# Reordering the last stage of an attention plus soft-mixture kernel: second-layer parts, their sums, output products and the copies between them

## The chip, the cores and the metric

The kernel runs on one core of one Trainium2 chip. The metric is the device time of one execution in microseconds (us), the median over repeated runs. The profile is that of one execution; its engines are PE (TensorE matmul), PEld (TensorE weight load), DVE (VectorE), ACT (ScalarE), POOL (GpSimd) and SP (SyncE), and 16 DMA engines move data between HBM and the core.

## The reference: what is computed

First an attention in both directions between 512 tokens and 32 states, for 8 batches and 8 heads of width 64; its results, 544 rows for each batch, make the 4608 x 512 matrix `x` of a soft mixture of experts:

```python
logits = x @ phi                        # 4608 x 32: 8 experts, 4 slots each
d = softmax of logits over the rows;  slot_input = d.T @ x      # 32 x 512
for e in range(8):
    h = np.maximum(slot_input[e] @ w1[e], 0.0)     # 4 x 1024
    slot_out[e] = h @ w2[e]                        # 4 x 512
c = softmax of logits over the 32 slots
return c @ slot_out                     # 4608 x 512
```

All data are 32-bit floats. `w1` and `w2` are 16 MB each, the tokens 8 MB, the output 9 MB.

## The kernel before, in words

The tokens and the weights are loaded whole, by 1 MB transfers that the SP engine issues one after the other on one queue, as buffers of the pool `big` come free. The attention stage is a long list of steps in a fixed order. Then come the experts. The first layer (`w1_part`, L679) issues the last weight transfers as it goes (`load_w`, `load_w2`, L115).

The change lies in what follows, the second layer and the output. The order in which PE, ACT, DVE and SP get their instructions is the order in which the steps are called, written by hand in the last block of the listing. Each engine takes its own instructions in that order and waits where an operand is not there.

- The 512 output columns fall into four parts `k` = 0 to 3 of 128 columns. Parts 0 and 1 need the weight tiles of half `c` = 0, parts 2 and 3 those of half `c` = 1, and the tiles of `c` = 1 arrive last. `more(k, n)` issues the next `n` of the 16 pieces of part `k`; a piece (`w2_part`, L745) is four matmuls for one expert and one half of the hidden width, and stands in the trace as 8 matmul records. All pieces of a part add up in one PSUM bank of the pool `ps_s`, which has two banks.
- `so_copy(k)` (L758) takes the finished part from PSUM to `so_sb`. `so_sum(k)` is one matmul (L763) that adds up four row groups, and an ACT copy of its result to `so_r` (L764).
- `out(k, q)`, for `q` = 0 and 1, makes four products of 128 x 512 (L774, 8 matmul records in all) in four PSUM banks, two of `ps_m` and two of `ps_t`; both pools have three banks. ACT copies the products 0 and 2 (L783), DVE the products 1 and 3 (L784), and SP sends the 1 MB tile to HBM, in one transfer (L789), or in two of 512 KB, each after its pair of copies (L787), for those in `HALVED`.
- `out_st(c)` (L796 to L805) does the same for the 256 KB of state rows of one half.

The queue of the transfers is the same for loads and stores: SP issues an output transfer after it has issued everything called before it and when the copies are done.

Of the kernel before, what the change touches and what calls it, by code (L numbers as in the profile page):

```python
# [8 lines left out]
F32 = mybir.dt.float32  # L9
# [6 lines left out]
P = 128  # L16
# [6 lines left out]
NJ = S // P  # L23
# [41 lines left out]
def attention_soft_moe(ctx: ExitStack, tc: tile.TileContext, x0, x, stT, phi, w1, w2, out_x, out_s):  # L65
# [7 lines left out]
    pe, act, dve, pool = nc.tensor, nc.scalar, nc.vector, nc.gpsimd  # L73
# [20 lines left out]
    for b in range(1, B):  # L94
        t = big.tile([P, 4, NJ, 2 * D], F32, tag="big", name=f"x{b}")
# [70 lines left out]
    with ExitStack() as actx:  # L166
        wk = actx.enter_context(tc.tile_pool(name="work", bufs=1))
        sm = actx.enter_context(tc.tile_pool(name="small", bufs=2))
        ps_s = actx.enter_context(tc.tile_pool(name="ps_s", bufs=2, space=PSUM))
        ps_t = actx.enter_context(tc.tile_pool(name="ps_t", bufs=3, space=PSUM))  # L170
        ps_m = actx.enter_context(tc.tile_pool(name="ps_m", bufs=3, space=PSUM))
# [10 lines left out]
        def half(name):  # L182
            return wk.tile([P, S], F32, tag="h", name=name, bufs=NH)
# [528 lines left out]
        c = [half(f"c{i}") for i in range(3)]  # L712
        c = [v[:, 0 : t.shape[1]].rearrange("p (t n) -> p t n", n=NS) for v, t in zip(c, c_t)]
# [23 lines left out]
        so, so_sb, so_r = {}, {}, {}  # L737
        PART = {k: (k // 2, P * (k % 2), P) for k in range(4)}

        def w2_part(k, hf, e):  # L740
            c, col, n = PART[k]
            if hf == 0 and e == 0:
                so[k] = ps_s.tile([P, n], F32, tag="sc", name=f"so_ps{k}")
            for i in range(4):
                pe.matmul(  # L745
                    so[k][32 * i : 32 * i + 32, :],
                    h_m[hf][:, 256 * i + 32 * e : 256 * i + 32 * e + 32],
                    w2t[c, e, 4 * hf + i][:, col : col + n],
                    start=(hf == 0 and e == 0),
                    stop=(hf == 1 and e == E - 1),  # L750
                )

        def so_copy(k):
            c, col, n = PART[k]
            if col == 0:
                so_sb[c] = half(f"so_sb{c}")[:, 0:256]
                so_r[c] = half(f"so_r{c}")[:, 0:256]
            dve.tensor_copy(so_sb[c][:, col : col + n], so[k])  # L758

        def so_sum(k):  # L760
            c, col, n = PART[k]
            p = ps_m.tile([P, n], F32, tag="ms", name=f"sum_ps{k}")
            pe.matmul(p, rep, so_sb[c][:, col : col + n], start=True, stop=True)  # L763
            act.copy(so_r[c][:, col : col + n], p)  # L764

        HALVED = ((0, 0), (3, 1))

        def out(k, q):
            hf, col = k // 2, 128 * (k % 2)
            o = [(ps_t if j % 2 else ps_m).tile([P, 512], F32, tag="tr" if j % 2 else "ms", name=f"o{k}_{q}_{j}")  # L770
                 for j in range(NJ)]
            for j in range(NJ):
                rows = slice(32 * j, 32 * j + 32)
                pe.matmul(  # L774
                    o[j],
                    so_r[hf][rows, col : col + 128],
                    lt_all[rows, 4 * q : 4 * q + 4, :].rearrange("p b s -> p (b s)"),
                    start=True,
                    stop=True,
                )  # L780
            ot = big.tile([P, NJ, 512], F32, tag="big", name=f"out{k}_{q}")
            for jp in range(2):
                act.copy(ot[:, 2 * jp], o[2 * jp])  # L783
                dve.tensor_copy(ot[:, 2 * jp + 1], o[2 * jp + 1])  # L784
                if (k, q) in HALVED:
                    half_rows = slice(1024 * jp, 1024 * jp + 1024)
                    nc.sync.dma_start(out_x[k, q][:, half_rows], ot[:, 2 * jp : 2 * jp + 2].rearrange("p i s -> p (i s)"))  # L787
            if (k, q) not in HALVED:
                nc.sync.dma_start(out_x[k, q], ot.rearrange("p i s -> p (i s)"))  # L789
# [39 lines left out]
        def more(k, n):  # L829
            for _ in range(n):  # L830
                w2_part(*part[k].pop(0))
# [5 lines left out]
        more(1, 4)  # L837
        more(0, 8)
        so_copy(0)
        more(1, 4)  # L840
        so_sum(0)
        more(1, 2)
        out(0, 0)
        more(1, 4)
        out(0, 1)
        more(1, 2)
        so_copy(1)
        more(2, 3)
        so_sum(1)
        more(2, 2)  # L850
        out(1, 0)
        more(2, 5)
        out(1, 1)
        more(2, 6)
        so_copy(2)
        more(3, 3)
        so_sum(2)
        out(2, 0)
        more(3, 5)
        out(2, 1)  # L860
        more(3, 8)
        so_copy(3)
        out_st(0)
        so_sum(3)
# [32 lines left out]
```

## Time and profile before

| what | value |
|---|---|
| device time, median of 3 runs | 131.25 us (131.04 to 131.4) |
| device time of the profiled execution | 131.05 us |
| its span, first to last instruction | 129.3 us |
| PE, DVE, ACT, POOL busy | 90%, 68%, 59%, 35% of the span |
| moved by DMA | 51.76 MB, mean 400 GB/s |
| read from and written to HBM | 42.53 MB and 8.91 MB |

The device time is 1.75 us longer than the span; this part lies outside what the profile shows. The busy shares are means over the whole span. The stage that the change touches runs from about 97 us to the end, and from 122.8 us on no compute engine works: there only transfers are left.

### The profile page before, as it was taken

Reading aid. Unit: us, or ns where it says so; the run is one execution under the profiler, and the core shown is the slowest. Engines: PE = TensorE matmul, PEld = TensorE weight load, DVE = VectorE, ACT = ScalarE, POOL = GpSimd, SP = SyncE. Lnnn points to the kernel's source line nnn. Section 1 sums busy time; section 2 is a strip of 40 time slices with the busy share of each in tenths; the row PEclk is TensorE's granted clock in tenths of the full one; section 3 lists DMA queues with packets and bytes.
Section 4 is the critical chain, followed back from the end, with each engine's and each line's share of the span. In section 5 each row is a group of like instructions: output and inputs, shape, how many; then the busy total and the mean of one; then the engine's idle time right before and its main releaser. Section 6 shows DMA issues by size and latency. Waiting matters only on the chain.

```text
span 129.3 us, 4981 instructions
## 1 busy us (share of the span) xinstructions
PE 116.3 (90%) x2112; PEld 82.1 (64%) x2112; DVE 88.1 (68%) x224; ACT 76.8 (59%) x187; POOL 45.2 (35%) x64
## 2 busy tenths in 40 slices
PE   6888999999999999999889899999999989898800
PEld 3527676869596976858676768963497546575300
DVE  3049999999999999999997349208950536263800
ACT  3118999999999999988985930410100425162700
POOL 2205393294575339057967113901600000000000
PEclk9999999999999999999999999999999999999965
DMA  4999999999999999999999999999999999989695
GB/s 104 382 415 426 428 423 426 421 421 426 413 431 423 421 428 421 434 416 428 418 426 423 423 403 404 402 434 423 426 421 428 423 409 397 416 325 423 287 404 214
DMA packets 8806, 51.76 MB, mean 400 GB/s; under 512 B 976, under 2 KB 1104, under 8 KB 3408
## 3 DMA queue, kind: packets, MB, share of 16 engines
q1 hardware_dynamic: 8640, 50.93, 95.3%
q10 hardware_dynamic: 144, 0.52, 1.1%
q8 instruction: 16, 0.26, 0.7%
q14 instruction: 6, 0.05, 0.1%
HBM read 42.53 MB, written 8.91 MB: 398 GB/s over the span
## 4 chain that ended last, share of the span: by engine, by line
PE 52%; DVE 32%; ACT 4%; DMA 3%; issue 3%; DVEq 0%; ACTq 0%
PE h_ps L679 11%; PE so_ps L745 11%; PE o L774 7%; PE xt_ps L232 5%; DVE q L260 5%; DVE aT L290 4%; DVE l1s L276 4%; DVE m L265 4%; DVE nm L296 4%; DMA x_a<-x_in 3%; PE sc L247 3%; PE eT_ps L315 2%; PE sr_ps L340 2%; DVE r L281 2%; PE t_ps L489 2%
## 5 line engine op out<-in xcount | busy, mean ns | idle before, releaser
L269 POOL TENSOR_TENSOR q<-q,m 128x512 f32<-128x512 f32 x16 | 16.7, 1049 | 16.1 <-DVE m L265 7.6
L238 ACT ACTIVATE xt<-xt_ps 128x512 f32<-128x512 f32 x30 | 17.9, 619 | 6.8 <-PE xt_ps L232 6.7
L285 POOL TENSOR_TENSOR q<-q,r 128x512 f32<-128x512 f32 x16 | 16.7, 1048 | 8.3 <-DVE r L281 2.7
L784 DVE COPY out<-o 128x512 f32<-128x512 f32 x16 | 10.3, 686 | 11.6 <-PE o L774 11.6
L745 PEld LDWEIGHTS so_ps<-w,h_m 128*32 128x32 f32 x512 | 13.6, 110 | 5.6 <-issue 5.3
L745 PE MATMUL so_ps<-w,h_m 128*32 128x128 f32 x512 | 16.2, 274 | 0.0
L232 PE MATMUL xt_ps<-ident,x 128*128 128x128 f32 x112 | 16.0, 277 | 0.0
L679 PE MATMUL h_ps<-w,si_m 128*32 128x512 f32 x128 | 14.4, 594 | 0.4 <-DVE si_m L643 0.4
L783 ACT COPY out<-o 128x512 f32<-128x512 f32 x16 | 8.6, 590 | 9.0 <-PE o L774 9.0
L232 PEld LDWEIGHTS xt_ps<-ident,x 128*128 128x128 f32 x112 | 12.4, 141 | 2.3 <-issue 0.8
L260 DVE STREAM_TRANSPOSE q<-sc 128x512 f32<-128x512 f32 x16 | 11.1, 694 | 1.1 <-PE sc L247 1.1
L679 PEld LDWEIGHTS h_ps<-w,si_m 128*32 128x32 f32 x128 | 9.1, 110 | 4.2 <-issue 2.6
L301 ACT ACTIVATE e<-sc,nm 128x512 f32<-128x512 f32 x16 | 11.3, 707 | 0.7 <-DVE q L260 0.4
L290 DVE STREAM_TRANSPOSE aT<-q 128x512 f32<-128x512 f32 x16 | 10.7, 687 | 0.2 <-PE sr_ps L340 0.2
L774 PE MATMUL o<-lt_all,so_r 32*128 32x512 f32 x64 | 9.9, 636 | 0.7 <-ACT so_r L764 0.7
L272 ACT ACTIVATE q<-q 128x512 f32<-128x512 f32 x16 | 10.5, 659 | 0.0
L276 DVE TENSOR_REDUCE l1s<-q 128x16 f32<-128x512 f32 x16 | 10.5, 655 | 0.1
L296 DVE TENSOR_REDUCE nm<-sc 128x1 f32<-128x512 f32 x16 | 10.5, 660 | 0.0
L265 DVE TENSOR_REDUCE m<-q 128x16 f32<-128x512 f32 x16 | 10.5, 658 | 0.0
L315 PE MATMUL eT_ps<-ident,e 128*128 128x128 f32 x64 | 9.9, 279 | 0.5 <-ACT e L301 0.5
L315 PE MATMUL an_ps<-ident,aT 128*128 128x128 f32 x64 | 9.9, 280 | 0.2 <-DVE aT L290 0.2
L332 ACT COPY an<-an_ps 128x512 f32<-128x512 f32 x16 | 9.7, 607 | 0.1
(134 smaller groups left out, 193.3 us busy)
## 6 DMA issues: line engine op xcount, KB each, us to landing
w<-w_in SPq DMA_DIRECT2D x30, 1024.0 KB, 19.4
x<-x_in SPq DMA_DIRECT2D x6, 1024.0 KB, 13.8
out_x<-out SPq DMA_DIRECT2D x6, 1024.0 KB, 5.1
out_x<-out SPq DMA_DIRECT2D x4, 512.0 KB, 5.5
x<-x_in SPq DMA_DIRECT2D x2, 512.0 KB, 6.3
w<-w_in SPq DMA_DIRECT2D x4, 256.0 KB, 12.1
w<-w_in SPq DMA_DIRECT2D x2, 512.0 KB, 7.6
x_a<-x_in ACTq DMA_DIRECT2D x1, 512.0 KB, 4.6
```

The source lines that it names most:

```text
L232: pe.transpose(p[:, P * j : P * j + P], xg[b, g][:, j, :], ident)
L238: scaled(r[f"xt{g}"], r[f"xp{g}"], 0.125)
L260: dve.transpose(r[f"q{h}"], r[f"sp{h}"])
L265: dve.tensor_reduce(out=r[f"m1{h}"], in_=r[f"qv{h}"], axis=AX.X, op=ALU.max)
L269: pool.tensor_tensor(v, v, R[b][f"m1{h}"].broadcast_to([P, 16, NS]), op=ALU.subtract)
L276: dve.tensor_reduce(out=l1s[:, i, :, 0:1], in_=R[b][f"qv{h}"], axis=AX.X, op=ALU.add)
L285: pool.tensor_tensor(v, v, R[b][f"r1{h}"].broadcast_to([P, 16, NS]), op=ALU.mult)
L290: dve.transpose(r[f"aT{h}"], r[f"q{h}"])
L315: pe.transpose(p[:, j, :], r[f"{src}{h}"][:, P * j : P * j + P], ident)
L679: pe.matmul(h_ps[hf][32 * kt : 32 * kt + 32, :], si_m[kt // 2][:, 256 * (kt % 2) + 32 * e : 256 * (kt % 2) + 32 * e + 32], w1t[hf, e, kt], ...
L745: pe.matmul(so[k][32 * i : 32 * i + 32, :], h_m[hf][:, 256 * i + 32 * e : 256 * i + 32 * e + 32], w2t[c, e, 4 * hf + i][:, col : col + n], ...
L774: pe.matmul(o[j], so_r[hf][rows, col : col + 128], lt_all[rows, 4 * q : 4 * q + 4, :].rearrange("p b s -> p (b s)"), start=True, stop=True,)
```

## The change

One copy (part 2) goes from DVE to ACT. `HALVED` splits the transfer of output (3, 0) in place of (0, 0). The last output (3, 1) takes the banks of its products 2 and 3 from `ps_s`. And the calls of the stage stand in another order: the sums of parts 1 and 2 come after more pieces of later parts, and three of the copies stand ahead of copies of output products that were ahead of them. No instruction is added or taken away, and the arithmetic is the same.

```diff
-            dve.tensor_copy(so_sb[c][:, col : col + n], so[k])
+            (act.copy if k == 2 else dve.tensor_copy)(so_sb[c][:, col : col + n], so[k])
...
-        HALVED = ((0, 0), (3, 1))
+        HALVED = ((3, 0), (3, 1))
...
-            o = [(ps_t if j % 2 else ps_m).tile([P, 512], F32, tag="tr" if j % 2 else "ms", name=f"o{k}_{q}_{j}")
-                 for j in range(NJ)]
+            homes = [(ps_m, "ms"), (ps_t, "tr")] * 2
+            if (k, q) == (3, 1):
+                homes[2:] = [(ps_s, "sc")] * 2
+            o = [pool.tile([P, 512], F32, tag=t, name=f"o{k}_{q}_{j}") for j, (pool, t) in enumerate(homes)]
...
         so_copy(0)
-        more(1, 4)
+        more(1, 6)
         so_sum(0)
         more(1, 2)
+        more(2, 3)
         out(0, 0)
+        more(2, 1)
         more(1, 4)
+        more(2, 1)
+        so_copy(1)
+        more(2, 1)
         out(0, 1)
-        more(1, 2)
-        so_copy(1)
+        more(2, 2)
+        so_sum(1)
         more(2, 3)
-        so_sum(1)
-        more(2, 2)
         out(1, 0)
         more(2, 5)
+        so_copy(2)
         out(1, 1)
-        more(2, 6)
-        so_copy(2)
-        more(3, 3)
+        more(3, 1)
         so_sum(2)
+        more(3, 4)
         out(2, 0)
         more(3, 5)
         out(2, 1)
-        more(3, 8)
+        more(3, 6)
         so_copy(3)
         out_st(0)
         so_sum(3)
```

## Rows read from the trace of the kernel before

**Rows 1.** Stretches: PE busy (x instructions), PE clock, DMA share, GB/s
```profile
108.20:109.10 0.90, 0.90 (x12) 1.00 0.82 337
109.10:113.90 4.80, 4.44 (x114) 1.00 0.99 415
113.90:115.40 1.50, 1.50 (x30) 1.00 0.58 229
...
120.90:121.30 0.40, 0.40 (x5) 1.00 0.33 123
121.30:122.00 0.70, 0.70 (x7) 1.00 0.06 23
122.00:122.20 0.20, 0.18 (x1) 1.00 1.25 532
```

**Rows 2.** Four single transfers: issue (duration in ns, start in us), landing
```profile
L115 SPq DMA_DIRECT2D w<-w_in x1: 328/328/328, 86.9 to 86.9; - x1
...
DMA to landing us min/median/max: 19.3/19.3/19.3
...
L789 SPq DMA_DIRECT2D out_x<-out x1: 332/332/332, 110.5 to 110.5; - x1
...
DMA to landing us min/median/max: 5.6/5.6/5.6
...
L789 SPq DMA_DIRECT2D out_x<-out x1: 332/332/332, 114.5 to 114.5; - x1
...
DMA to landing us min/median/max: 4.8/4.8/4.8
...
L805 SPq DMA_DIRECT2D out_s<-out_s x1: 1209/1209/1209, 123.5 to 123.5; - x1
...
DMA to landing us min/median/max: 4.7/4.7/4.7
```

**Rows 3.** Instruction queue's transfers, 98:122 and 114:115.5: count, MB, engines' time
```profile
q8 instruction: 4, 0.07, 1.0%
...
q8 instruction: 1, 0.02, 5.4%
```

**Rows 4.** Timeline of PE: start, us, instructions, idle before and releaser
```profile
98.64 0.49 PE L763 MATMUL sum_ps<-so_sb,rep 128*128 128x128 f32 x2
99.06 0.65 PE L745 MATMUL so_ps<-w,h_m 128*32 128x128 f32 x16
99.64 1.14 PE L774 MATMUL o<-lt_all,so_r 32*128 32x512 f32 x8
100.71 1.22 PE L745 MATMUL so_ps<-w,h_m 128*32 128x128 f32 x32
...
104.69 0.46 PE L763 MATMUL sum_ps<-so_sb,rep 128*128 128x128 f32 x2 [0.46 <-DVE so_sb L758]
...
109.03 2.17 PE L745 MATMUL so_ps<-w,h_m 128*32 128x128 f32 x72
111.13 0.49 PE L763 MATMUL sum_ps<-so_sb,rep 128*128 128x128 f32 x2
111.98 1.14 PE L774 MATMUL o<-lt_all,so_r 32*128 32x512 f32 x8 [0.36 <-ACT so_r L764]
...
117.23 0.70 PE L796 MATMUL os<-lts_all,so_r 32*128 32x256 f32 x4
```

**Rows 5.** Timelines of DVE and ACT, copies of the stage
```profile
103.06 1.29 DVE L784 COPY out<-o 128x512 f32<-128x512 f32 x2 [0.94 <-PE o L774]
...
113.18 1.29 DVE L784 COPY out<-o 128x512 f32<-128x512 f32 x2 [2.27 <-PE o L774]
...
119.91 2.60 DVE L784 COPY out<-o 128x512 f32<-128x512 f32 x4 [1.48 <-PE o L774]
...
111.66 0.27 ACT L764 COPY so_r<-sum_ps 128x128 f32<-128x128 f32 x1 [1.47 <-PE sum_ps L763]
...
121.66 0.59 ACT L783 COPY out<-o 128x512 f32<-128x512 f32 x1 [0.23 <-PE o L774]
```

## The prediction

> **What bounds the kernel now.** I read the page first: PE is busy for 90% of the span, but the DMA line is at 9 in nearly all slices, and the last slices hold transfers alone. So I went on to the stretches of the last 25 us, with their share of the DMA engines [rows 1]. The reader is to see that the 16 engines are full (share 0.99 from 109.1 to 113.9), that they run short at four places, and that one of them, from 121.3 to 122.0, has a share of 0.06, which is one engine in sixteen: fifteen have nothing to do and one still works. At 122.0 to 122.2 the share goes up again: the next output has come.
>
> The single transfers [rows 2] give the clock of the last engine. A transfer has landed when its last part has. The last weight tile lands at 86.9 + 19.3 = 106.2, output (1, 1) at 110.5 + 5.6 = 116.1, output (2, 0) at 114.5 + 4.8 = 119.3, and the last state rows at 123.5 + 4.7 = 128.2. Between 106.2 and 116.1 four outputs of 1 MB went out one behind the other: 9.9 / 4 = 2.48 us for 1 MB, without a gap. From 106.2 to the end 8 outputs and two times 0.25 MB are to be written, 8.5 MB, so 8.5 x 2.48 = 21.05 us for an engine that never waits; it took 22.0. The engine that ends last has thus lost only 0.95 us: 119.3 - 116.1 - 2.48 = 0.7 at output (2, 0), and 128.2 - 119.3 - 3.5 x 2.48 = 0.2 behind it, around 122.0.
>
> The mean over the engines tells another story. The idle shares of [rows 1] are 0.9 x 0.18 = 0.16, 1.5 x 0.42 = 0.63, 0.4 x 0.67 = 0.27 and 0.7 x 0.94 = 0.66, in all 1.7 us. But most of it is idle time of engines that were early and waited for outputs while the late ones still worked; each engine has its own share of every transfer, and the early ones can't take work from the late. [...] By the mean the change could give back 1.7 us, by the last engine at most 0.95; the share of 0.06 agrees with the second.
>
> What makes an engine late? In the stretch from 114 to 115.5 the instruction queue moved one block of 16 KB, which took 5.4% of 16 engines for 1.5 us, that is 1.3 us of one engine; the four blocks between 98 and 122 took 1.0% of 24 us x 16, 0.96 each [rows 3]. The block at 114 stands just ahead of the 0.7 us that output (2, 0) is late. [...]
>
> **The change part by part.** *PE's order.* From start to start [rows 4]: a sum takes 99.06 - 98.64 = 0.42 us, two pieces 99.64 - 99.06 = 0.58, nine pieces 111.13 - 109.03 = 2.10, so n pieces take 0.14 + 0.22 n; an output's products take 100.71 - 99.64 = 1.07. The waits are 0.46 at the sum of part 1 (DVE is at two output copies, 103.06 to 104.35 [rows 5], before it copies part 1) and 0.36 at output (2, 0), where nothing stands between the sum of part 2 and its use and PE waits for ACT's copy. The new order from there: sum 0 at 98.64 + 2 x 0.22 = 99.08, output (0, 0) at 100.74 (five pieces), (0, 1) at 103.49 (seven), sum 1 at 105.14, output (1, 0) at 106.36, (1, 1) at 108.67, sum 2 at 110.10, output (2, 0) at 111.54, (2, 1) at 113.85, and the state rows' products at 116.38 instead of 117.23. PE gains 0.85 us, the two waits. Output (0, 0) comes 1.1 and (0, 1) 1.6 us later than now.
>
> *Covers.* The copy of part 1 fits between DVE's copies for (0, 0), which end at 103.2, and those for (0, 1), which can start at 104.7. The copy of part 2 on ACT costs about 0.27 us (the 128 x 128 copy in [rows 5]) and falls at about 108.8, while ACT has no other work until 109.8: ACT idles 1.47 before its copy at 111.66 now. Without that cover the products of (1, 1) would come 0.27 later. Pieces of part 2 now start at 100 instead of 104: the last piece needs the weight tile that lands at 106.2, and is reached at 108.4. Bank reuse adds no wait: each bank taken was copied out at least 0.4 us before by these times.
>
> *The last output in three pools.* ACT's idle 0.23 before 121.66 goes away, but DVE copies the four odd products of (3, 0) and (3, 1) without a break, 2.60 us from 119.91 [rows 5]. So the end of the copies moves only with PE, by 0.85; the banks by themselves give nothing. Bounds: 0 and 0.23.
>
> *The split moves from (0, 0) to (3, 0).* The number of transfers stays. Splitting lets half of an output go one DVE copy (0.65) earlier. At (0, 0) the loss of this is hidden: the late engines are at weights until about 105.8, and the whole output is there at 104.2.
>
> *Do the late engines ever wait?* An output is issued when DVE ends its copies, 113.18 + 1.29 = 114.47 against 114.5 [rows 2, 5], which is 2.49 after PE began its products (111.98), and the engines start about 0.9 later: the share comes back at 115.4 [rows 1]. So the new outputs are ready for the engines 3.4 us after PE's times above: (0, 0) at 104.2, (0, 1) 106.9, (1, 0) 109.8, (1, 1) 112.1, (2, 0) 114.9, (2, 1) 117.2. The last engine wants them about 0.4 before the landing of the one ahead (it ended at 122.0 what landed at 122.4): 105.8, 108.3, 110.8, 113.2, 115.7, 118.2. The state rows (0.25 MB, wanted at 120.6) are 0.85 earlier than now and ready at 118.5. The first half of (3, 0) is issued at 119.91 + 0.65 - 0.85 = 119.7, so ready at 120.6 against 121.3 wanted; its second half and (3, 1) follow by 0.65 each while one half takes 1.24. So the last engine waits nowhere; the smallest margin is 0.7 us. Were the split not moved, (3, 0) would be ready at 121.2, with no margin.
>
> **The sum.** The 0.2 us around 122 comes back wholly. Of the 0.7 at (2, 0) I take 0.5. The block of instructions at 114 is still fetched. It cost its engine between 1.3 us [rows 3] and 1.3 + 0.7 = 2.0, where it is followed by the slow start of (2, 0). The engines that ran dry first were free up to 1.5 us before the last (from 113.9 to 115.4 [rows 1]). If the block hits one of these, as it seems to have done, that engine ends between 1.5 - 1.3 = 0.2 ahead of the late chain and 2.0 - 1.5 = 0.5 behind it. I take 0.2 behind, nearer to the plain block time. The gain is 0.95 - 0.2 = 0.75 us, about 0.7: 131.05 - 0.7 = 130.35 for the profiled execution. That one lies 0.2 below the median of 131.25, so 130.4 is my number; bounds of this case 131.05 - 0.95 = 130.1 and 131.05 - 0.45 + 0.2 = 130.8.
>
> **The rivals.** *All the idle time comes back.* If engines could share the work, or if the late ones were late only because of the gaps, 1.7 us: 131.05 - 1.7 = 129.35. For it speaks that the copies stop being late everywhere; against it, the one engine that works on alone.
>
> *The block costs the end as much as now.* Then only the 0.2 around 122 comes back: 130.85. The 0.85 that PE gains is lost to engines that wait for nobody. For it: the same blocks are fetched by the same number of instructions.
>
> *Slower: a block hits a late engine.* If the new order shifts the fetch to an engine that is already last, its whole price is added to a chain without gaps: 106.2 + 21.05 + 2.0 = 129.25 instead of 128.2, so 131.05 + 1.05 = 132.1. It decides from a price of 0.95 us upwards. Against it: of the four blocks of the stretch, only one shows in the late chain now.
>
> **How the numbers follow.** My forecast has 0.55 (130.4, from 130.1 to 130.8), all idle back 0.10 (129.35), block as now 0.27 (130.85), slower 0.08 (132.1). A change of 0.3%, 0.4 us, is about what a measurement of this kernel can tell from none. Faster by more, below 130.86: nearly all of the first, the second, and some 0.1 of the third, which stands on the border: 0.73. Slower, above 131.64: 0.07. Within: 0.20. The range reaches from the second case to just above no change, 129.3 to 131.3; the slower case is left out.
>
> **What would show it right or wrong.** Right: PE does not idle before the sum of part 1 and before (2, 0), and the state rows' products start at 116.4, give or take 0.3; the DMA share stays near 1 from 106 to about 124 and then falls in steps, because early engines end first, instead of the sharp end of now; (2, 0) and (2, 1) land 2.5 us apart and the last transfer at 127.3 to 127.7. Wrong on the size: the share falls to 0.06 for a time at the very end, with an instruction block a few us before. Wrong altogether: a gap of the share to nothing before the end (an output came too late after all), a wait of PE for a weight tile of `c` = 1, or the last landing before 127.

## The result and the profile after

The changed kernel takes 132.91 us (132.84 to 133.03) against 131.31 for the kernel before in the same measurement: a ratio of 1.0126, 95% interval [1.0109, 1.0144]. It is slower by 1.6 us, where I forecast 0.85 us less. The profiled execution took 132.84 us with a span of 131.0, where I forecast 130.35.

Two points of the description of the change are to be set right, as the argument uses them. Two copies move ahead of copies of output products, those of parts 1 and 2, and not three. And the sum of part 2 comes after fewer pieces of part 3 than before (one in place of three); what is new is that four pieces then stand between it and output (2, 0).

The timeline of PE in the last stage of the changed kernel, and the one row of PEld, the weight loads, at the same place (columns as in [rows 4]):

```profile
99.79 0.64 PE L745 MATMUL so_ps<-w,h_m 128*32 128x128 f32 x14
101.11 1.03 PE L745 MATMUL so_ps<-w,h_m 128*32 128x128 f32 x26 [0.68 <-issue]
102.07 1.14 PE L776 MATMUL o<-lt_all,so_r 32*128 32x512 f32 x8
...
104.81 1.14 PE L776 MATMUL o<-lt_all,so_r 32*128 32x512 f32 x8
...
107.66 1.14 PE L776 MATMUL o<-lt_all,so_r 32*128 32x512 f32 x8
...
117.64 0.70 PE L798 MATMUL os<-lts_all,so_r 32*128 32x256 f32 x4
```
```profile
101.11 0.76 PEld L745 LDWEIGHTS so_ps<-w,h_m 128*32 128x32 f32 x25 [0.95 <-issue]
```

The two waits of [rows 4], 0.46 and 0.36 us, are gone. In their place PE stands still at 100.2, for 0.68 us by PE's row, whose ends are modelled, and 0.95 by PEld's, in the middle of pieces; the releaser is "issue", so nothing that the profile shows was waited for. From this place on every step comes 1.3 us later than I had added up: output (0, 0) at 102.07 and not 100.74, (1, 0) at 107.66 and not 106.36, the state rows' products at 117.64 and not 116.38. Of the 1.3, 0.3 is a later start of the whole stage (the first layer starts at 78.1 instead of 77.8; that differs by some tenths from run to run: the state rows' products come at 118.10 in `after_again`, the same kernel), and 1.0 is this wait. It uses up the 0.85 us of the two old ones.

The stretches of the end, first two of the kernel before, which continue [rows 1], then those of the changed kernel (the columns are length, PE clock, DMA share, GB/s):

```profile
122.20:127.80 5.60, 0.61 0.98 402
127.80:129.30 1.50, 0.50 0.00 0
```
```profile
103.00:105.60 2.60, 1.00 0.63 262
...
110.80:111.50 0.70, 1.00 0.26 105
111.50:114.00 2.50, 1.00 1.03 426
114.00:115.40 1.40, 1.00 0.95 392
115.40:120.80 5.40, 1.00 1.02 428
...
127.80:128.60 0.80, 0.50 0.17 67
...
129.20:129.70 0.50, 0.50 0.06 25
```

The dry stretches, in which engines are out of work, have moved from the end to the beginning: engines wait for the first output (103 to 105.6), nearly all of them again before (1, 0) (110.8 to 111.5), and hardly any behind that. And the end is no longer sharp. At 127.8, where before all sixteen ended together, thirteen end; 0.17 of sixteen, some three engines, go on, and the last one (0.06) until 129.7. Most engines end when they did before; the loss lies in these three.

The single transfers say where the last landings got late (as in [rows 2]: last weight tile, outputs (0, 0), (0, 1), (1, 1), and the last state rows):

```profile
L115 SPq DMA_DIRECT2D w<-w_in x1: 328/328/328, 87.2 to 87.2; - x1
DMA to landing us min/median/max: 19.3/19.3/19.3
...
L791 SPq DMA_DIRECT2D out_x<-out x1: 351/351/351, 104.6 to 104.6; - x1
DMA to landing us min/median/max: 4.4/4.4/4.4
L791 SPq DMA_DIRECT2D out_x<-out x1: 343/343/343, 107.4 to 107.4; - x1
DMA to landing us min/median/max: 5.4/5.4/5.4
...
L791 SPq DMA_DIRECT2D out_x<-out x1: 332/332/332, 112.5 to 112.5; - x1
DMA to landing us min/median/max: 6.4/6.4/6.4
...
L807 SPq DMA_DIRECT2D out_s<-out_s x1: 1120/1120/1120, 124.1 to 124.1; - x1
DMA to landing us min/median/max: 5.9/5.9/5.9
```

Landings: 87.2 + 19.3 = 106.5 for the weights, 109.0, 112.8, 118.9, and 130.0 at the end. That is 23.5 us from the weights to the end, where 8.5 MB need 21.05: by the landings 2.4 us are lost, where 0.95 were lost before. From (0, 0) to (0, 1) it takes 3.8 us instead of 2.48, that is 1.3 too long; to (1, 1), two outputs further, 6.1 instead of 4.96, 1.1 too long. In both places the instruction queue moved a block, in the trace one packet of 16 KB, of which each kernel's page has 16 (0.26 MB) (stretches 107.5 to 110.5 and 114 to 116.5, where the shares are 1.15 and 0.96 us of one engine):

```profile
q8 instruction: 1, 0.02, 2.4%
```

Whether the blocks sit on the late engines can be read from the trace itself, which holds the start and length of every packet. During both blocks sixteen packets are under way (median), fifteen of data and the block, so the block has one engine to itself. A packet of 8 KB takes 0.31 us (the median of 999 behind 100 us), and where an engine works alone it starts the next without a gap: eight packets of 84 ns follow one another at steps of 80 from 129.04 to 129.69. So an engine can be followed back from its last packet. The one that ends last, at 129.7, comes without a break to the block at 114.73. It was about 0.7 us behind most engines there; the block took 0.96 us and the first packet behind it 0.67, and with its share of (1, 1) it is done at 118.5, most engines at 116.4. The engine that ends third (128.4) comes to the block at 108.28 (1.14 us, then a packet of 0.72). At 114.7 their packets are 14 ns apart, so one engine may have had both blocks. The second (129.0) had no block: between 113 and 118 us its packets take up to 0.40 us, for a reason that the trace doesn't show.

### The profile page after: what moved, and what is told of

It is laid out like the page before. It is cut to its first block, busy times and chain, and to the rows that moved or that the text cites. A ratio compares the mean times of both kernels' runs of the same rounds, so it can differ in the third digit from the quotient of the medians.

```text
span 131.0 us, 4980 instructions
## 1 busy us (share of the span) xinstructions
PE 116.5 (89%) x2112; PEld 81.7 (62%) x2112; DVE 87.9 (67%) x223; ACT 76.9 (59%) x188; POOL 45.2 (35%) x64
## 4 chain that ended last, share of the span: by engine, by line
PE 45%; DVE 33%; DMA 5%; issue 4%; ACT 3%; SPq 2%; POOL 0%; DVEq 0%; ACTq 0%; POOLq 0%
PE so_ps L745 12%; PE h_ps L679 11%; PE o L776 6%; DMA phi_sb<-phi_in 5%; DVE l1s L276 5%; DVE aT L290 5%; DVE q L260 5%; DVE m L265 4%; DVE nm L296 4%; PE xt_ps L232 3%; PE sc L247 3%; DVE r L281 2%; PE eT_ps L315 2%; PE sr_ps L340 2%; DVE out L786 2%
## 5 line engine op out<-in xcount | busy, mean ns | idle before, releaser
L323 ACT COPY eT<-eT_ps 128x512 f32<-128x512 f32 x16 | 9.6, 610 | 0.6 <-PE eT_ps L315 0.3
```

## The experiments

Fourteen runs in four groups; each group had the kernel before beside it on the same chip, and each ratio is to that. The theories, as they came up: A, PE's wait and the late first outputs make the loss; B, the unsplit (0, 0) makes it; C and D, engines that instruction blocks make late set the end, whatever the outputs do; F and G part A into the wait alone and the order alone.

### Order without split and banks; first output earlier; blocks cut elsewhere

`order_only`: the changed kernel with the old split and old banks.

```diff
-        HALVED = ((3, 0), (3, 1))
+        HALVED = ((0, 0), (3, 1))
...
-            if (k, q) == (3, 1):
-                homes[2:] = [(ps_s, "sc")] * 2
```

> The new order of calls and the copy of part 2 on ACT, but the split of output (0, 0) and the banks of the last output as before. Theory A (the order itself makes the first outputs late: PE runs into the end of its fetched instructions at 100.2 us, waits 0.95 us there, and all engines then run dry before output (1, 0)): as slow as the changed kernel, 132.6 to 133.1 us, with the same wait. Theory B (output (0, 0) in one piece starts the stores too late): back to 131.0 to 131.6 us.

132.54 us, 1.0106 [1.0091, 1.0121], with PE's wait at the same place (0.82 us, to 101.0). Theory B falls: with (0, 0) split as before it is nearly as slow. The order carries most of the loss.

`early00`: output (0, 0) ahead of the first three pieces of part 2.

```diff
-        more(2, 3)
         out(0, 0)
-        more(2, 1)
+        more(2, 4)
```

> The changed kernel, but output (0, 0) comes ahead of the first three pieces of part 2. Its 1.07 us of products then stand ahead of the instruction at which PE waited. Theory A: no wait of PE there (under 0.2 us), outputs (1, 0) and later ones 0.8 to 1.0 us earlier, no dry stretch of the DMA engines before output (1, 0), 131.0 to 131.9 us. Theory B: (0, 0) is still in one piece but 1.6 us earlier, also faster, 131.5 to 132.3 us, with the wait of PE where it was. A third theory C (one engine made late by an instruction block near 114.7 us sets the end by itself): no better than 132.5 us.

132.94 us, 1.017 [1.0115, 1.0226]. It missed its aim: the wait is still there (0.68 us, to 101.0), now just ahead of output (0, 0), since the place lies two matmul records ahead of the products and not, as I had counted, behind them. Theory C (no better than 132.5) is met. Of A the run tells only that the wait stays at one place of PE's instruction stream and not at one step.

`after_pad48` and `before_pad8`: tiny matmuls added to the turning of the tokens in the attention stage.

```diff
+            for _ in range(2 if b < 4 else 1):                 # before_pad8: 1 if b == 1 or b == 3 else 0
+                pe.matmul(p[0:32, 0:32], ident[0:32, 0:32], ident[0:32, 0:32], start=True, stop=True)
             for j in range(NJ):
                 pe.transpose(p[:, P * j : P * j + P], xg[b, g][:, j, :], ident)
```

> The changed kernel with 48 added tiny matmuls (32 x 32, 192 PE instructions) spread over the attention stage, so that the blocks of instructions are cut at other places; the order of the last stage is untouched. Theory A: the wait of 0.95 us at the 3521st PE instruction goes, or moves and shrinks below 0.5 us; output (1, 0) is issued 0.5 to 1 us earlier; 131.2 to 132.3 us. Theory B: 132.7 to 133.2 us.

> The kernel before with 8 added tiny matmuls (32 PE instructions) in the attention stage: the end of the fetched block moves from just behind output (0, 0) to the dense pieces ahead of it. Theory A: a wait of PE of 0.7 to 1.1 us there, which the kernel before does not have, output (0, 0) that much later; the time the same or up to 0.8 us longer, 131.2 to 132.0 us, as the queue still holds weights then. Theory B: no such wait, 131.0 to 131.4 us.

With 48 of them the attention stage itself grew by 10 us (first layer at 87.9), 141.19 us, and the time says nothing on the question; the wait had gone (40 records of pieces run through between the first sum and the first output in 1.30 us). With 8 of them, 133.86 us, 1.0212 [1.0168, 1.0257], longer than either theory had it; 1.1 us of it is the attention stage (first layer at 79.0). Here the kernel before, in its own order, has the wait too. The timeline of its PE:

```profile
100.21 0.64 PE L747 MATMUL so_ps<-w,h_m 128*32 128x128 f32 x15
101.74 0.27 PE L747 MATMUL so_ps<-w,h_m 128*32 128x128 f32 x1 [0.89 <-issue]
101.94 1.14 PE L776 MATMUL o<-lt_all,so_r 32*128 32x512 f32 x8
```

It stands one matmul record ahead of output (0, 0). In the kernel before, the same place of the instruction stream (counted under `after_less`) lies six records behind the products, 15 records later in the order; the added instructions are 16 records of PE and 16 of PEld, so they shift it by about that. The packets say the rest. In each of the ten traces with a wait of 0.4 us or more at this place, by the starts of PE's and PEld's records, PE goes on 1.3 to 1.5 us after the transfer of one instruction block has ended: 99.67 and 101.11 in the changed kernel, 100.25 and 101.74 here. My reading is that PE had come to the end of its fetched instructions; no view shows what PE had at hand, only these times and the place.

### First output as before; the tail alone; three splits; fewer instructions

`first0_split3`: the order as before up to output (0, 0), the copy of part 1 ahead of output (0, 1), that of part 2 on ACT but behind output (1, 1) as before, the sum of part 2 two pieces ahead of its use, three outputs split, new banks.

```diff
-        HALVED = ((3, 0), (3, 1))
+        HALVED = ((0, 0), (3, 0), (3, 1))
...
-        more(1, 6)
+        more(1, 4)
         so_sum(0)
         more(1, 2)
-        more(2, 3)
         out(0, 0)
-        more(2, 1)
-        more(1, 4)
-        more(2, 1)
+        more(1, 6)
         so_copy(1)
-        more(2, 1)
         out(0, 1)
         more(2, 2)
         so_sum(1)
         more(2, 3)
         out(1, 0)
         more(2, 5)
-        so_copy(2)
         out(1, 1)
+        more(2, 6)
+        so_copy(2)
         more(3, 1)
         so_sum(2)
-        more(3, 4)
+        more(3, 2)
         out(2, 0)
         more(3, 5)
         out(2, 1)
-        more(3, 6)
+        more(3, 8)
```

> The order of before up to and with output (0, 0), so that its products stand ahead of the 3521st PE instruction; then the rest of part 1, its copy ahead of output (0, 1), and two pieces between the sum of part 2 and output (2, 0). Outputs (0, 0), (3, 0) and (3, 1) split, banks of the changed kernel. Theory A (late first outputs and the wait of PE make the loss): no wait of PE over 0.2 us at that place, first output issued at 101.6 us, no dry stretch before output (1, 0), 130.2 to 131.2 us. Theory D (the end is that of an engine hit by an instruction block after the last dry stretch, whatever the outputs do): 131.6 to 132.8 us.

> The version with the first output as before and three split outputs, once more with more rounds, for its ratio to the kernel before: both theories by now 0.994 to 1.000.

130.84 us, 0.9973 [0.9943, 1.0002]; once more with more rounds, 130.74 us against 131.56, 0.9932 [0.9906, 0.9958]. The second interval is clear of one: it beats the kernel before, and on the same chip the changed kernel (132.65 us, `after_again`). Theory D alone had it at 131.6 or more, so D falls in its strict form: the outputs do matter. The stretches of `first0_again`:

```profile
103.00:105.60 2.60, 1.00 0.99 403
...
114.00:115.40 1.40, 1.00 0.63 246
...
120.80:121.50 0.70, 1.00 0.54 214
...
127.00:127.80 0.80, 0.50 0.03 10
```

The queue is full at the beginning, the dry stretches are late again, and the end is sharp, at 127.0 to 127.3. The last two blocks start at 109.55 and 114.29 us here, the second one in a dry stretch.

`tail_only`: the kernel before with the split of (3, 0) for (0, 0) and the new banks.

> The kernel before with the split moved from (0, 0) to (3, 0) and the new banks of the last output; order and copies as before. Theory A: output (3, 0) starts 0.65 us earlier, the dry stretch at 121 to 122 shrinks by that, 130.5 to 131.0 us; the unsplit (0, 0) costs nothing while weights are still in the queue. Theory B (the unsplit (0, 0) is what costs): 131.6 to 132.9 us. Theory D: the engine that lands (2, 0) late is no longer waited for, gain of at most 0.3 us.

131.51 us, 1.0006 [0.9978, 1.0034]: no difference. Theory B falls once more, and the tail's changes by themselves bring nothing that shows; A had put it lower, D (at most 0.3) fits.

`after_split3`: the changed kernel with (0, 0) split as well.

```diff
-        HALVED = ((3, 0), (3, 1))
+        HALVED = ((0, 0), (3, 0), (3, 1))
```

> The changed kernel with (0, 0) split too, so three outputs in halves. Theory B: back to 131.3 us or less. Theory A: first half 0.65 us earlier, the dry stretch before (1, 0) stays, 132.3 to 132.9 us. Theory D: 132.5 to 133.0 us.

132.31 us, 1.0087 [1.0054, 1.0119]. It lies at the lower edge of A; an earlier half output helps a little, if at all, the order's loss stays.

`after_less`: 284 instructions fewer in the attention stage, by single matmuls of the whole output in `G`, `U`, `V` and `Px`.

> The changed kernel with 284 PE instructions fewer in the attention stage: the logits of the states' part, the turned states and four products of the running sum are each replaced by one matmul of the same output size, so its output is another. [...] Theory D: the wait of PE near 100 us stays, no block after 110 us, and the last engine ends within 1.4 us of the first instead of 2.0: 131.6 to 132.3 us. Theory A: 132.5 to 133.0 us, less what the attention stage may save.

133.93 us, 1.0207 [1.0164, 1.0249], against both theories. The attention stage got 1.1 us longer (first layer at 79.2), and a block was still fetched at 115.4, so it did not take away the late block, as it was meant to. What it did show is in the count of records up to the wait, PE and PEld, in the changed kernel and in this one (stretches from 0; the numbers behind x are the records):

```profile
0.00:100.60 100.60, 95.85 (x1744) 69.81 (x1745) 76.42 (x203) 66.80 (x166) 45.24 (x64) 1.00 0.99 409
```
```profile
0.00:101.70 101.70, 96.82 (x1616) 69.01 (x1617) 76.62 (x203) 67.00 (x166) 45.15 (x64) 1.00 0.99 408
```

3489 records, and 3233: exactly 256 fewer. In `order_only` and `early00`, too, the count at the wait is 3489 (3491 in `before_pad8`). The kernel before has 3489 behind it at 100.87 and goes on at 100.9, 1.5 us after its block was in (99.34), so without a wait.

### A delay ahead of the last outputs

14 dummy transposes between the sum of part 3 and output (3, 0), in the changed kernel and in the kernel before.

```diff
         so_sum(3)
+        spin_(14)
         out(3, 0)
```

> The changed kernel with 14 dummy transposes (about 1.5 us of PE, 1.1 us beyond the wait that is there anyway) between the sum of part 3 and output (3, 0): both last outputs and the last state rows come 1.1 us later. Theory D (the end is that of one to three engines that instruction blocks have made up to 2 us late, and these have work until 123.7 us): no more than 0.3 us longer than the changed kernel on the same chip, 132.7 to 133.2 us; the mass of the engines ends 1.1 us later, the last one where it did. Theory A (the outputs' arrival sets the end): 1.0 to 1.2 us longer, 133.9 to 134.2 us.

> The kernel before with the same 14 dummy transposes at the same place. There all engines wait for output (3, 0) at 122 us, so both theories give 1.0 to 1.2 us more: 132.1 to 132.6 us. It shows that the delay has its full price where the engines wait.

> The changed kernel itself, beside the others on the same chip: 132.8 to 133.1 us, ratio 1.011 to 1.015.

By the medians on this chip: the kernel before 131.56, with the delay 133.32, 1.0132 [1.0101, 1.0163], so 1.8 us more; the changed kernel 132.65, 1.0093 [1.0066, 1.0121], with the delay 133.26, 1.0157 [1.0117, 1.0196], so 0.6 us more. That is between D (up to 0.3) and A (1.0 to 1.2), and the runs of one kernel are up to 1.7 us apart here, so the medians decide for neither. The profiled executions, one of each kernel, are clearer. First the changed kernel with the delay, then the kernel before with it:

```profile
122.00:123.20 1.20, 1.00 0.37 150
...
127.80:128.60 0.80, 0.50 1.00 392
128.60:128.90 0.30, 0.50 0.18 62
...
129.20:129.70 0.50, 0.50 0.06 25
```
```profile
122.00:123.20 1.20, 1.00 0.00 0
...
128.60:128.90 0.30, 0.50 0.98 382
...
129.20:129.70 0.50, 0.50 0.00 0
```

In the changed kernel most engines now wait at 122 to 123 and end at 128.7 instead of 127.8, but the last one ends at 129.7 as without the delay. In the kernel before all wait, and all end 1.2 us later (129.1). So in this execution the last engine of the changed kernel does not wait for the last outputs at all; its packets follow one another without a gap from the instruction block at 114.17 on. It is behind with earlier outputs, as D has it.

### The first output at its old place, and a delay put in behind it

`after_first0`: sum of part 0 and output (0, 0) at their old place, all else of the changed kernel kept; `after_first0_wait`: 9 dummy transposes added.

```diff
-        more(1, 6)
+        more(1, 4)
         so_sum(0)
         more(1, 2)
-        more(2, 3)
         out(0, 0)
+        more(1, 2)
+        more(2, 3)
+        spin_(9)               # only in after_first0_wait
         more(2, 1)
```

> The changed kernel with the sum of part 0 and output (0, 0) back at their old place (four pieces of part 1, sum, two pieces, output), all the rest of its order, its split and its banks kept: its products again stand ahead of the 3521st PE instruction, and output (0, 1) starts at 103.5 us, (1, 0) at 106.4 us, as in the prediction. Theory F (the wait of PE alone makes the loss): no wait there over 0.3 us, no dry stretch before (1, 0), 130.2 to 131.2 us, ratio 0.99 to 0.998. Theory G (the order alone makes it, since (0, 1) and (1, 0) come later than before also without the wait): a dry stretch before (0, 1) or (1, 0), engines late to the end, 131.6 to 132.6 us, ratio 1.004 to 1.012.

> The same with 9 dummy transposes, 0.96 us of PE, ahead of the pieces after output (0, 0): the lost wait is put back at nearly its old place, with output (0, 0) still early. Theory F: the loss is back, ratio 1.008 to 1.015. Theory G: 0.2 to 0.5 us more than without it, ratio 1.006 to 1.015, so it is the difference between the two that tells: over 0.8 us for F, under 0.5 us for G.

132.47 us, 1.0073 [1.0042, 1.0105], and with the dummies 133.11 us, 1.0113 [1.0072, 1.0155]. Theory F falls: over half of the loss is still there. The dummies add 0.6 us, between F and G, and the intervals overlap. But the pair doesn't part wait and order cleanly, as `after_first0` isn't free of the wait. PE's row behind output (0, 0):

```profile
100.71 0.42 PE L745 MATMUL so_ps<-w,h_m 128*32 128x128 f32 x6
101.32 2.78 PE L745 MATMUL so_ps<-w,h_m 128*32 128x128 f32 x90 [0.19 <-issue]
104.03 1.14 PE L776 MATMUL o<-lt_all,so_r 32*128 32x512 f32 x8
```

The gap is 0.46 us by PEld's row, at the same 3489 records, and it ends 1.5 us after the block was in (99.81). Output (1, 0) starts at 107.09, not at the 106.4 expected. The stretches of `after_first0`:

```profile
110.00:110.80 0.80, 1.00 0.31 123
...
127.00:127.80 0.80, 0.50 0.33 128
...
128.60:128.90 0.30, 0.50 0.07 27
```

Most engines end at 127.2, half a microsecond ahead of the kernel before; the last one ends at 129.0. Followed back, it comes to the block at 113.66. There is a dry stretch before (1, 0) here too, whose copies on DVE end at 109.6 while SP issues the transfer at 110.0.

## Why the prediction was wrong

**The bound was read rightly.** The last engine and not the mean over the engines sets the end: one engine at 129.7, with the last landing at 130.0, while thirteen are done at 127.8, and these took nothing of its share: the eight packets of 2 KB from 129.04 on are its sixteenth of the last 256 KB, as are the eight from 121.33 to 121.97 in the kernel before. And in the profiled executions the delay costs most engines 0.9 us and the last one nothing.

**The step that failed is the term of the instruction block, "I take 0.2 behind".** Its price was about right: I had 1.3 to 2.0 us for the engine that it hits, and the block at 114.7 with the slow packet behind it cost 1.3. What was wrong is the credit of 1.5 us against it, for an engine that had run dry early. That credit is the dry stretch of the kernel before (113.9 to 115.4 [rows 1], share 0.58, in which its block at 114.13 falls), and all its engines waited again at 122, where whoever was late caught up. The prediction has the new outputs ready in time, so that nobody waits, and still spends the idle time of the old order. The lone engine of 121.3 to 122.0, followed back, comes to a packet of 1.29 us that starts 14 ns after the end of that block: it was late there too, and the wait at 122 hid it. In the changed kernel the share from 111.5 to 120.8 is 0.95 to 1.03: the block falls on an engine with work behind it, and nothing follows in which it could catch up. By the landings 2.4 us are lost where I had 0.2; with the 0.3 of the later start that is the whole miss of 2.5 us.

The rival that a block hits a late engine had 0.08. It was what happened, and as the rule: in ten traces of the new order and its variants the engine that ends last, followed back, comes to a late instruction block (in `after_split3` it is the last but one, 0.06 us ahead of the last). It ends 1.1 to 2.0 us behind most engines there; in the kernel before, with the delay too, it is 0.1, in the two traces of the version that won 0.3 and 0.6, and there the dry stretches lie late. The rival's 132.1 us was itself 0.7 short of the 132.84: 0.3 for the later start, and 2.4 lost where it had 2.0. The sign that I had named for a wrong size, a share of 0.06 at the very end, is there (129.2 to 129.7).

**PE's order was costed by durations alone.** The 0.85 us of the two waits did come back, and were lost to a wait of 0.95 us that no row of before shows, since there PE comes to the place at 100.87 just when it can go on. Ahead of this place the kernel before had output (0, 0), 1.07 us for 8 matmul records; the change put pieces there, 0.22 us for 8. By the counts the wait comes 256 records earlier in `after_less`, after 3233 in place of 3489. What was paid in the last stage of the changed kernel is 0.95 us of PE at this place, and 0.9 to 1.1 us of a DMA engine for each of its four blocks from 98 us on.

**"The last engine waits nowhere" rested on too small a margin.** Outputs (0, 1) and (1, 0) were to be ready at 106.9 and 109.8, 1.4 and 1.0 us before the last engine wants them. With the later start (0.3), PE's wait (0.95) and an issue that SP made 0.4 after the copies (109.6 and 110.0 in `after_first0`; 110.15 and 110.6 in the changed kernel) they came at about 108.2 and 111.5, and nearly all engines ran dry.

**Right** were: that the moved split and the banks decide nothing (`tail_only`), and that PE would not wait at the sum of part 1 and at (2, 0). Most engines end at 127.2 in `after_first0`, near what I had for the last one, but that is another kernel.

**Open.** How much PE's wait adds: `after_first0` has half of it, and the pair's intervals overlap. Why the last engine was 0.7 us behind most already ahead of the block at 114.7, why the first packet behind a block takes 0.7 us in place of 0.31, and why the second engine had slow packets, no run shows. And no run took a late block away alone: that the last engine had it is in the traces, what the kernel would take without it is not measured.

## What to carry to other kernels

Where a queue of stores ends a kernel, ask which engine ends last and what lets it catch up: the stretch in which all engines waited for the producer, here at 122 us, also hid how late one of them was (0.7 us of work alone, 121.3 to 122.0), and the order that filled it ended with one engine 1.9 us behind most (127.8 and 129.7). The version that won, `first0_split3`, keeps the first outputs early and the dry stretches late, and gains 0.3 and 0.7% in its two measurements; it differs from `after_first0`, which lost, in the place of output (0, 1), in later steps and in one split, and these were not taken apart. And before dense matmuls are moved together, count instructions as well as microseconds: here, with pieces (0.22 us for 8 records) in place of products (1.07), PE had 3489 records behind it at 100.2, 0.5 us after the transfer of a block had ended (99.67), and stood still until 101.1; in the kernel before it came there at 100.87, 1.5 us after its block (99.34), and did not wait.

## What was not expected of the hardware

PE stood still 0.65 to 0.89 us by its own row after 3489 records of its stream in the changed kernel, `order_only` and `early00`, after 3491 in `before_pad8`, and after 3233, 256 earlier, where the program was shorter by 284 instructions (`after_less`). In the changed kernel it passed its 3233rd record at 96.1, had the 3489th behind it at 100.2, and went on at 101.1, 5.0 us after the first.

While the block at 114.7 was fetched, one of the sixteen engines carried no data, for 0.96 us, with a packet of 0.67 us in place of 0.31 behind it.

Tiny instructions of PE in the attention stage, meant as padding, cost 1.1 us (32 of them) and 10 us (192); 284 fewer, with larger matmuls in place of small ones, cost 1.1 us as well. That stage's times move with PE's stream in a way that was not followed up.
